# Attention inside a transformer block: the first 160 queries of a weighted sum moved ahead of the third score product, and the accumulator copied in pieces of 160 and 352

## The chip, the cores and the metric

The kernel runs on one core of one Trainium2 chip. The core has a matrix engine (TensorE, in the profile PE, with its weight loads as PEld), VectorE (DVE), ScalarE (ACT), GpSimd (POOL) and SyncE (SP), which issues transfers. Each works off its own list of instructions in order, and waits for the others through semaphores. The metric is the device time of one execution in microseconds. Lower is better.

## What is computed

```
def _A_ref(x, wqkv, wo):                 # B=1, S=2048, D=512
    H = 32; Dh = D // H                  # 32 heads of 16
    q, k, v = ...                        # (x @ wqkv), by heads
    scores = einsum("bhqd,bhkd->bhqk", q, k) * Dh ** -0.5
    p = softmax(scores, axis=-1)
    o = einsum("bhqk,bhkd->bhqd", p, v)
    return o.transpose(0, 2, 1, 3).reshape(B, S, D) @ wo

h  = x + _A_ref(_layernorm(x))
h2 = h + _B_ref(_layernorm(h))           # a gated MLP with a 2048x2048 mix of the rows
```

The change lies in the attention, between the projections and `@ wo`.

## The kernel before

The attention stage goes through *units*: one group of four heads (`hg`, 8 of them), one block of 512 queries (`qb`, 4) and one block of 128 keys (`kb`, 16). Two units make a *pair*, the body of the main loop (line 1044, `n` in steps of two), 256 pairs in all. The first 246 follow a fixed order, the list `PAIR` of line 40 (the last of them without the products M below); the others, at the end of the stage, take another branch.

A pair interleaves three streams on TensorE:

- **Score products s0 to s7** (line 804): transposed scores of one head, 128 keys by 512 queries, into one of three `s` buffers in PSUM (the matrix engine's accumulation memory). ScalarE takes the exponential of each into `pt` (line 813). With three buffers, a score product needs the exponential of the third one before it to have ended. s0 to s3 belong to the first unit, s4 to s7 to the second, each by two head pairs and two heads. They run in the order s0, s2, s1, s3, s5, s4, s6, s7.
- **Products for the row maxima M0 to M7** (line 223): the same scores the other way round, for a block of queries some eleven pairs ahead. Softmax needs each row's maximum before its exponentials. They run in the order M0, M4, M1, M2, M3, M5, M7, M6 and take four PSUM banks in turn, `m0` to `m3`, by `count[0] % 4`: M0 and M3 share the first, M4 and M5 the second, M1 and M7 the third, M2 and M6 the fourth. VectorE takes the maximum of each (line 228), but M3's absolute value is taken by ScalarE (line 233) and joined with M6's on VectorE (line 237, one instruction that adds and takes the maximum).
- **Weighed sums** (`weigh`, line 824): the exponentials times the values, into the accumulator `pv`, one PSUM bank of 128 rows and 512 queries, as four products side by side, one for each head, in 32 columns of the array each. The fp32 operands make each product two passes, so a group of four shows as eight instructions. `P` is the sum of the pair's first unit, all 512 queries, at the end of the pair. The sum of the second unit follows in the next pair in two halves of 256 queries, both called `H` in the list (H1 and H2 below); it reads the exponentials of s4 to s7 of the previous pair.

A *boundary pair* is the first of a block of queries (`kb == 0`). After its H2 the accumulator holds the finished block. At the token `out` the function `take` (line 836) copies it on VectorE to `og` in SBUF and sends it to memory in two transfers. P of the same pair begins the next block in the same bank. 30 boundary pairs run the list `PAIR`; the first pair of all has no block before it.

Three tokens do smaller things: `join` (the maxima of a finished block are put together, on VectorE and GpSimd), `turn` (they are transposed on VectorE and go through memory into the queries' tile, three transfers, line 255) and `invert` (the reciprocal of the sums of a block, line 772). Each comes once in eight pairs, none in a boundary pair.

TensorE, ScalarE, VectorE, GpSimd and SP keep the order in which the program names their instructions, so the list is the order of TensorE's queue. The framework places the waits.

Of the kernel before, what the change touches and what calls it, by code (L numbers as in the profile page):

```python
# [8 lines left out]
F32 = mybir.dt.float32  # L9
# [6 lines left out]
AX = mybir.AxisListType  # L16
# [3 lines left out]
P = 128  # L20
# [16 lines left out]
FIRST = 2  # L37
RG = 64
VW = DH + 1
PAIR = "s0 M0 join s2 M4 M1 s1 H s3 invert M2 s5 M3 H out M5 s4 M7 turn s6 s7 M6 P".split()  # L40
HF = 3 * P
FC = FH // 2
LOW = -3.0e38
# [16 lines left out]
def block_kernel(ctx: ExitStack, tc: tile.TileContext, x, wqkv, wo, w_in, w_sp4, b_sp, w_out, out):  # L60
# [134 lines left out]
                    qst[g][RG * t + j:RG * t + KS:3, :, :],  # L195
                    q_scr[(0, 1, 0)[j], h0:h0 + 2 * DH, c].rearrange("(p r) s -> r p s", r=DH))

    more = {}

    def bank(i):  # L200
        if i in more:
# [3 lines left out]
    def max_pair(m):  # L205

        g, i = divmod(m, 8)
        hg, qb = divmod(g, NQ)
        q, k, w = qst[g], kst[hg % 2], uvs[hg % 2]
        if i == 0:
            mx[g] = sm.tile([P, 16, 4], F32, name="mx")
            nc.gpsimd.memset(mx[g][:, :8, 3:], LOW)
        c, p = slice(i % 4 * P, i % 4 * P + P), i // 4
        at = lambda t, e: mx[g][:, t * 8 + i, e:e + 1]

        def scores(t, keys, b):  # L220
            r = slice(RG * t, RG * t + KS)
            acc = bank(b)
            nc.tensor.matmul(acc, q[r, p, c], keys[r, p], start=True, stop=True)  # L223
            return acc

        def one(t, e, b):
            acc = scores(t, k[:, :, 512 * e:512 * e + 512], b)
            nc.vector.reduce_max(at(t, e if t else e - 1), acc, axis=AX.X)  # L228

        def minus(b):  # L230
            acc = scores(0, w[:, :, 512:], b)
            ab[0] = sm.tile([P, 512], F32, name="ab")
            nc.scalar.activation(ab[0], acc, AF.Abs)  # L233

        def plus(b):
            acc = scores(0, w[:, :, :512], b)
            nc.vector.tensor_tensor_reduce(ab[0], acc, ab[0], 0.5, LOW, ALU.add, ALU.max, at(0, 0))  # L237

        def finish():
            if i == 7:  # L240
                nm = sm.tile([P, 2, 8], F32, name="nm")
                nc.vector.tensor_reduce(nm.rearrange("p t i -> p (t i)"), mx.pop(g), axis=AX.X,  # L242
                                        op=ALU.max, negate=True)
                parts = sm.tile([P, 2, 2, 8], F16, name="mparts")
                nc.gpsimd.tensor_scalar(nm, nm, 1.0 / ONE, 1.0, op0=ALU.mult, op1=ALU.mult)  # L245
                nc.gpsimd.tensor_copy(parts[:, :, 0], nm)
                nc.gpsimd.tensor_sub(parts[:, :, 1], nm, parts[:, :, 0])
                turned[0] = (g, parts)

        ab = {}  # L250
        four = [lambda b, e=e: one(1, e, b) for e in range(4)]
        two = [lambda b, e=e: one(0, e, b) for e in (2, 3)]
        return [four[0], two[0], two[1], minus, four[1], four[2], plus, four[3], finish]

# [532 lines left out]
    with ExitStack() as at:  # L787
# [36 lines left out]
        def weigh(hg, qb, kb, a=0, b=512):  # L824
            if kb == 0:
                pv[0] = ps_v.tile([P, 512], F32, name="pv")
            for j in range(4):
                c = (4 * kb + j) * VW
                nc.tensor.matmul(pv[0][32 * j:32 * j + 32, a:b], vst[hg % 2][:, c:c + 32],  # L829
                                 pts[j % 2, kb][:, j // 2, a:b], start=kb == 0, stop=kb == NB - 1,  # L830
                                 skip_group_check=True)
            if b == 512:
                for p in range(2):
                    del pts[p, kb]

        def take(hg, qb, pool=sm):

            o = pool.tile([P, 512], F32, name="og", bufs=2)
            nc.vector.tensor_copy(o, pv[0])  # L839
            for t in range(2):  # L840
                nc.sync.dma_start(four_heads(o_scr, hg)[t, :, :, qb * 512:qb * 512 + 512],
                                  o[64 * t:64 * t + 64])
# [201 lines left out]
        for n in range(0, len(units), 2):  # L1044
            (hg, qb, kb), (_, _, kb1) = units[n:n + 2]
            if m % 8 and n < 480:
                work(4.1 if m % 8 < 7 else 2.0)
            if n == 480:
                work(None)
            if hg + 1 < HG and n % 64 < 24 and n % 4 == 0:  # L1050
                load_k(hg + 1, [n % 64 // 4])
            if hg + 1 < HG and n % 64 < 12 and n % 4 == 2:
                load_uv(hg + 1, [n % 64 // 4])
            if hg + 1 < HG and n % 64 == 30:
                copy_v = load_v(hg + 1)
            if hg + 1 < HG and n % 64 == 36:
                copy_v()
            if kb == 2 and n // NB + 3 < HG * NQ:
                load_q(n // NB + 3)
            steps = max_pair(m) if m < 8 * HG * NQ else []  # L1060
            m += 1
            if not steps and not later:
                maxima.close()
                later.append(attn.enter_context(
                    tc.tile_pool(name="ps_l", bufs=1, space=PSUM, side="right")))
                steps_h.append(make_h(h_rows[0], later[0].tile([P, 512], F32, name="h")))
            elif not steps and len(later) == 1:
                inner.close()
                later.append(at.enter_context(tc.tile_pool(name="ps_t", bufs=2, space=PSUM)))
            ends = kb == 0 and n  # L1070

            def join():
                if joins:
                    joins.pop()()

            def some_h(k):
                for _ in range(k):
                    if steps_h and next(steps_h[0], True):
                        steps_h.pop()

            if kb == 2 and n > NB:
                gather_sums(*units[n - 3][:2])
            if len(later) == 2:
                if turned:
                    max_rows()
                more_h = n in (492, 494, 508, 510)
                scores2(hg, qb, kb, 0)
                scores2(hg, qb, kb, 1)
                some_h(1 + more_h)
                weigh(*prev)  # L1090
                if ends:
                    take(*prev[:2])
                scores2(hg, qb, kb1, 0)
                scores2(hg, qb, kb1, 1)
                some_h(1)
                weigh(hg, qb, kb)
            first = True
            for tok in PAIR if len(later) < 2 else ():
                i = int(tok[-1]) if tok[-1].isdigit() else 0
                if tok[0] == "s":  # L1100
                    score(hg, qb, (kb, kb1)[i // 4], i % 4 // 2, i % 2)
                elif tok[0] == "M" and steps:
                    steps[i](count[0] % 4)
                    count[0] += 1
                    if i == 6:
                        joins.append(steps[8])
                elif tok == "join":
                    join()
                elif tok == "H" and prev is None:
                    if first:  # L1110
                        pv[0] = ps_v.tile([P, 512], F32, name="pv")
                        for j in range(4):
                            nc.tensor.matmul(pv[0][32 * j:32 * j + 32, :], vst[0][:, :32],
                                             vst[0][:, :512], start=True, stop=True)
                    first = False
                elif tok == "H":
                    a = 0 if first else 256
                    weigh(*prev, a, a + 256)
                    first = False
                elif tok == "P":  # L1120
                    weigh(hg, qb, kb)
                elif tok == "out" and ends:
                    take(*prev[:2])
                elif tok == "invert" and kb == 6 and n > NB:
                    invert()
                elif tok == "turn" and turned:
                    max_rows()
            prev = (hg, qb, kb1)
            if len(later) == 2 and kb == 6:
                invert()  # L1130
            if n in (474, 484, 504, 508):
                asked.append(load_o(h_rows[{474: 0, 484: 1, 504: 2, 508: 3}[n]]))
            if n in (484, 492, 508):
                asked.pop(0)()
            if len(later) == 1 or n in (498, 510):
                split_o(h_rows[{498: 1, 510: 2}.get(n, 0)], False)
            if n == 500:
                steps_h.append(make_h(h_rows[1], later[0].tile([P, 512], F32, name="h")))
            if n == 502:
                new_hn(h_rows[0])  # L1140
# [458 lines left out]
```

## Time and profile before

| | us |
|---|---|
| three runs | 1713.01, 1713.76, 1713.85; median 1713.76 |
| the profiled execution | 1713.42 |
| its span, first to last instruction | 1711.6 |
| busy: PE, DVE, ACT, POOL | 1699.2, 1452.3, 1317.3, 811.9 |

The profiled execution has 1.8 us around its span. The granted clock of TensorE is full all along. The page divides the span into 40 slices of 42.8 us; these lines give the busy share of each in tenths, and the attention in the order of `PAIR` is the stretch from the fifth to the 29th:

```profile
DVE  7688999999999999999999999999936787543444
ACT  4334999999999999999999999999995545211111
PEclk9999999999999999999999999999999999999999
```

A row of a group names line, engine, operation, output and inputs and how often, then the busy time and the mean duration of one in ns, then the engine's idle time before them and what ended it. A row of a timeline gives the start in us from the span's beginning, the duration in us, engine, line and operation, and the count of those that follow one another. Durations on one engine overlap: the next instruction starts while the last is still finishing, so the step from start to start (or from end to end) is what one more instruction costs. The ends of matrix products are modelled.

### The profile page before, as it was taken

Reading aid. Unit: us, or ns where it says so; the run is one execution under the profiler, and the core shown is the slowest. Engines: PE = TensorE matmul, PEld = TensorE weight load, DVE = VectorE, ACT = ScalarE, POOL = GpSimd, SP = SyncE. Lnnn points to the kernel's source line nnn. Section 1 sums busy time; section 2 is a strip of 40 time slices with the busy share of each in tenths; the row PEclk is TensorE's granted clock in tenths of the full one; section 3 lists DMA queues with packets and bytes.
Section 4 is the critical chain, followed back from the end, with each engine's and each line's share of the span. In section 5 each row is a group of like instructions: output and inputs, shape, how many; then the busy total and the mean of one; then the engine's idle time right before and its main releaser. Section 6 shows DMA issues by size and latency. Waiting matters only on the chain.

```text
span 1711.6 us, 36671 instructions
## 1 busy us (share of the span) xinstructions
PE 1699.2 (99%) x13499; PEld 643.8 (38%) x13499; DVE 1452.3 (85%) x3051; ACT 1317.3 (77%) x2584; POOL 811.9 (47%) x1062
## 2 busy tenths in 40 slices
PE   9999999999999999999999999999999999999999
PEld 4533222222222222222222222222225666656665
DVE  7688999999999999999999999999936787543444
ACT  4334999999999999999999999999995545211111
POOL 1231867776673267687667776400002766300100
PEclk9999999999999999999999999999999999999999
DMA  5534332332221244344434444300114454664551
GB/s 185 163 98 142 105 89 67 102 94 81 82 66 24 57 118 117 98 150 126 130 113 123 132 140 130 80 13 19 37 39 124 139 174 139 235 234 156 199 216 44
DMA packets 189309, 196.03 MB, mean 115 GB/s; under 512 B 67496, under 2 KB 140008, under 8 KB 189128
## 3 DMA queue, kind: packets, MB, share of 16 engines
q1 hardware_dynamic: 186824, 188.04, 37.1%
q10 hardware_dynamic: 2304, 5.64, 0.8%
q8 instruction: 106, 1.74, 0.4%
q14 instruction: 75, 0.61, 0.1%
HBM read 122.10 MB, written 65.93 MB: 110 GB/s over the span
## 4 chain that ended last, share of the span: by engine, by line
PE 77%; DVE 13%; DMA 3%; POOL 3%; SPq 2%; ACT 1%; issue 1%; DVEq 0%; ACTq 0%; POOLq 0%
PE pv L829 26%; PE s L804 17%; PE m L223 9%; DVE mx L228 7%; PE g L108 4%; PE g L109 4%; PE g L107 4%; PE acc L107 4%; PE acc L109 3%; PE acc L108 3%; DMA rc<-r_scr 2%; DVE ab L237 1%; DVE og L839 1%; SPq L722 1%; DMA raw<-in_w_sp 1%
## 5 line engine op out<-in xcount | busy, mean ns | idle before, releaser
L813 ACT ACTIVATE pt<-s 128x512 f32<-128x512 f32 x1968 | 1007.1, 638 | 4.7 <-PE m L223 3.6
L228 DVE TENSOR_REDUCE mx<-m 128x1 f32<-128x512 f32 x1510 | 946.8, 681 | 11.8 <-PE m L223 2.9
L804 PE MATMUL s<-qst,kst 50*128 50x512 f16 x2048 | 604.2, 379 | 0.2
L829 PE MATMUL pv<-pt,vst 128*32 128x256 f32 (+1 forms) x6056 | 598.2, 466 | 4.0 <-DVE og L839 1.3
L223 PE MATMUL m<-kst,qst 48*128 48x512 f16 x1510 | 452.3, 381 | 0.0
L804 PEld LDWEIGHTS <-kst 50*128 50x128 f16 x2048 | 131.8, 94 | 352.0 <-issue 322.8
L829 PEld LDWEIGHTS pv<-pt,vst 128*32 128x32 f32 x6056 | 119.5, 108 | 289.4 <-issue 276.1
L223 PEld LDWEIGHTS <-qst 48*128 48x128 f16 x2048 | 159.3, 93 | 174.2 <-issue 124.6
L223 PE MATMUL m<-uvs,qst 48*128 48x512 f16 x504 | 190.7, 380 | 0.0
L245 POOL TENSOR_SCALAR nm<-nm 128x16 f32<-128x16 f32 x32 | 6.5, 203 | 358.3 <-DVE nm L242 358.3
L237 DVE CUSTOM_DVE_ANT_0 ab<-m,ab 128x512 f32<-128x512 f32 x252 | 170.2, 675 | 2.7 <-ACT ab L233 2.7
L233 ACT ACTIVATE ab<-m 128x512 f32<-128x512 f32 x252 | 157.8, 626 | 15.6 <-PE m L223 14.8
L1367 ACT ACTIVATE pr<-pr,up 128x304 f32<-128x304 f32 (+1 forms) x32 | 17.0, 574 | 108.5 <-DVE up L1321 108.5
L990 POOL TENSOR_TENSOR op<-raw,op 128x512 f16<-128x512 f32 x80 | 92.8, 1160 | 6.1
L913 POOL TENSOR_TENSOR raw<-raw 128x512 f32<-128x512 f32 (+1 forms) x84 | 83.1, 989 | 6.7
L918 POOL TENSOR_TENSOR acc_sp<-acc_sp,raw 128x512 f32<-128x512 f32 x63 | 80.3, 1275 | 4.5
L109 PE MATMUL acc<-wi,hT 128*128 128x344 f16 x256 | 79.1, 309 | 0.3 <-DVE hT L104 0.3
L107 PE MATMUL acc<-wi,hT 128*128 128x344 f16 x256 | 79.1, 309 | 0.0
L108 PE MATMUL acc<-wi,hT 128*128 128x344 f16 x256 | 79.1, 309 | 0.0
L1506 POOL TENSOR_TENSOR pr<-pr,z 128x344 f32<-128x344 f32 x8 | 7.3, 910 | 145.9 <-DMA whole<-squares 108.3
L910 POOL TENSOR_SCALAR raw<-raw 128x512 f32<-128x512 f32 (+1 forms) x88 | 52.1, 592 | 19.7 <-DMA raw<-in_wqkv 12.4
L1505 DVE TENSOR_TENSOR pr<-g,v 128x344 f32<-128x344 f32 x8 | 4.1, 516 | 66.6 <-PE g L109 63.5
(247 smaller groups left out, 2288.5 us busy)
## 6 DMA issues: line engine op xcount, KB each, us to landing
raw<-in_w_sp SPq DMA_DIRECT2D x128, 256.0 KB
s_scr<-op SPq DMA_DIRECT2D x64, 256.0 KB
op<-s_scr SPq DMA_DIRECT2D x32, 512.0 KB
a_scr<-op SPq DMA_DIRECT2D x48, 256.0 KB
op<-a_scr SPq DMA_DIRECT2D x24, 512.0 KB
o_scr<-og SPq DMA_DIRECT2D x64, 128.0 KB
qst<-q_scr SPq DMA_DIRECT2D x192, 32.0 KB
kst<-k_scr SPq DMA_DIRECT2D x48, 128.0 KB
```

Source lines behind the costliest of these rows:

```text
L107: nc.tensor.matmul(ps, lh, rh, start=first, stop=False, **kw)
L108: nc.tensor.matmul(ps, lh, rl, start=False, stop=False, **kw)
L109: nc.tensor.matmul(ps, ll, rh, start=False, stop=last, **kw)
L223: nc.tensor.matmul(acc, q[r, p, c], keys[r, p], start=True, stop=True)
L228: nc.vector.reduce_max(at(t, e if t else e - 1), acc, axis=AX.X)
L233: nc.scalar.activation(ab[0], acc, AF.Abs)
L237: nc.vector.tensor_tensor_reduce(ab[0], acc, ab[0], 0.5, LOW, ALU.add, ALU.max, at(0, 0))
L804: nc.tensor.matmul(s, kst[hg % 2][r, p, kb * P:(kb + 1) * P], qst[hg * NQ + qb][r, p, :], start=True, stop=True)
L813: nc.scalar.activation(pts[p, kb][:, t, :], s, AF.Exp, scale=scales_[hg // 2])
L829: nc.tensor.matmul(pv[0][32 * j:32 * j + 32, a:b], vst[hg % 2][:, c:c + 32], pts[j % 2, kb][:, j // 2, a:b], start=kb == 0, stop=kb == NB - 1,
L913: pool.tensor_mul(got[0] if n else acc, got[0], got[0])
L990: chores.append((lambda: pool.tensor_sub(t[0][:, 1], of(), t[0][:, 0]), TT))
```

## The change

Four edits.

- The list: the first part H1 goes from behind s1 to ahead of it, directly behind s2 and M4; M1 goes from ahead of s1 to behind it; `turn` goes from behind M7 to ahead of M5, and `invert` from behind s3 to behind `turn`.
- The two parts of the second unit's sum are 160 and 352 queries instead of 256 and 256, in every pair.
- In a boundary pair the accumulator is copied in two pieces: 160 queries directly behind H1, 352 at `out` behind H2. The transfers follow the second piece.
- In a boundary pair the maximum of M2 is held: it is not issued behind its product but behind the second piece, at `out`.

```
-PAIR = "s0 M0 join s2 M4 M1 s1 H s3 invert M2 s5 M3 H out M5 s4 M7 turn s6 s7 M6 P".split()
+PAIR = "s0 M0 join s2 M4 H s1 M1 s3 M2 s5 M3 H out turn invert M5 s4 M7 s6 s7 M6 P".split()
...
         def one(t, e, b):
             acc = scores(t, k[:, :, 512 * e:512 * e + 512], b)
-            nc.vector.reduce_max(at(t, e if t else e - 1), acc, axis=AX.X)
+            to = at(t, e if t else e - 1)
+            if hold:
+                held.append(lambda: nc.vector.reduce_max(to, acc, axis=AX.X))
+            else:
+                nc.vector.reduce_max(to, acc, axis=AX.X)
...
-        def take(hg, qb, pool=sm):
-
-            o = pool.tile([P, 512], F32, name="og", bufs=2)
-            nc.vector.tensor_copy(o, pv[0])
+        def take(hg, qb, pool=sm, a=0, b=512):
+
+            if not a:
+                pv[1] = pool.tile([P, 512], F32, name="og", bufs=2)
+            o = pv[1]
+            nc.vector.tensor_copy(o[:, a:b], pv[0][:, a:b])
+            if b < 512:
+                return
...
                 elif tok[0] == "M" and steps:
+                    if ends and i == 2:
+                        hold.append(1)
                     steps[i](count[0] % 4)
+                    hold.clear()
...
                 elif tok == "H":
-                    a = 0 if first else 256
-                    weigh(*prev, a, a + 256)
+                    weigh(*prev, *((0, 160) if first else (160, 512)))
+                    if ends and first:
+                        take(*prev[:2], a=0, b=160)
                     first = False
...
                 elif tok == "out" and ends:
-                    take(*prev[:2])
+                    take(*prev[:2], a=160)
+                    while held:
+                        held.pop(0)()
```

More of the change, by code (lines that the diff above doesn't have):

```diff
@@ L196, in load_q @@
                     q_scr[(0, 1, 0)[j], h0:h0 + 2 * DH, c].rearrange("(p r) s -> r p s", r=DH))
-    more = {}
+    more, hold, held = {}, [], []
     def bank(i):
```

## Prediction

> **What bounds the kernel now.** I read the page first (its groups), then the attention stage, pair by pair, in the timelines of ScalarE, TensorE and VectorE. In the groups, ScalarE's exponentials and VectorE's maxima are the two largest:
>
> ```profile
> L813 ACT ACTIVATE pt<-s 128x512 f32<-128x512 f32 x1968 | 1007.1, 638 | 4.7 <-PE m L223 3.6
> L228 DVE TENSOR_REDUCE mx<-m 128x1 f32<-128x512 f32 x1510 | 946.8, 681 | 11.8 <-PE m L223 2.9
> 197.47:1227.36 1029.89, 1025.96 (x9282) 291.50 (x9280) 1022.06 (x1984) 1028.59 (x2089) 613.10 (x809) 1.00 0.33 91
> ```
>
> The last row is a window that begins at one first exponential of a boundary pair and ends at another, 232 pairs later: 1029.89/232 = 4.439 us a pair. Its busy columns are TensorE, weight loads, VectorE, ScalarE, GpSimd; all three main engines look full, so the shares do not tell which one sets the pace. Single rows do. Durations overlap (an operation starts before the last has ended), so I compare ends. A regular pair, its first and its last exponential:
>
> ```profile
> 783.33 0.66 ACT L813 ACTIVATE pt<-s 128x512 f32<-128x512 f32 x1
> 783.82 0.66 ACT L813 ACTIVATE pt<-s 128x512 f32<-128x512 f32 x1
> 787.74 0.66 ACT L813 ACTIVATE pt<-s 128x512 f32<-128x512 f32 x1
> ```
>
> The first row is the last exponential (s7) of the pair before and ends at 783.99; s0 ends at 784.48, this pair's s7 at 788.40. Eight operations lie between the last two (seven exponentials and one absolute value), so (788.40 - 784.48)/8 = 0.49 us each, and the step 783.99 to 784.48 is 0.49 too. Nine times 0.49 is 4.41: in a regular pair ScalarE finishes one operation every 0.49 us without a hole. **ScalarE is the bound**, and no order of the others makes a regular pair shorter than 4.41. ScalarE loses time only around a boundary, where a new block of queries begins:
>
> ```profile
> 769.88 0.66 ACT L813 ACTIVATE pt<-s 128x512 f32<-128x512 f32 x1
> 770.56 0.60 ACT L813 ACTIVATE pt<-s 128x512 f32<-128x512 f32 x1
> 774.39 0.69 ACT L813 ACTIVATE pt<-s 128x512 f32<-128x512 f32 x1
> 775.06 0.60 ACT L813 ACTIVATE pt<-s 128x512 f32<-128x512 f32 x1
> ```
>
> These are s7 of the boundary pair, s0 of the next pair, that pair's s7, and the s0 after it. Ends 770.54 to 771.16 are 0.62 apart, 775.08 to 775.66 are 0.58: 0.13 and 0.09 more than 0.49. So a boundary costs 0.22 us, and the 30 boundaries that run this order cost 6.6 us. That is all that the reordered stage can give back. Why they cost it is seen on TensorE and VectorE:
>
> ```profile
> 765.55 0.39 PE L804 MATMUL s<-qst,kst 50*128 50x512 f16 x1
> 766.19 0.37 PE L804 MATMUL s<-qst,kst 50*128 50x512 f16 x1
> 767.06 0.39 PE L804 MATMUL s<-qst,kst 50*128 50x512 f16 x1
> 767.29 0.38 PE L804 MATMUL s<-qst,kst 50*128 50x512 f16 x1
> 767.60 0.64 PE L829 MATMUL pv<-pt,vst 128*32 128x256 f32 x8
> 768.64 0.39 PE L223 MATMUL m<-uvs,qst 48*128 48x512 f16 x1
> 769.14 1.07 PE L829 MATMUL pv<-pt,vst 128*32 128x512 f32 x8
> 770.14 0.39 PE L804 MATMUL s<-qst,kst 50*128 50x512 f16 x1
> 766.01 0.69 DVE L228 TENSOR_REDUCE mx<-m 128x1 f32<-128x512 f32 x1
> 766.61 0.68 DVE L228 TENSOR_REDUCE mx<-m 128x1 f32<-128x512 f32 x1
> 767.21 0.68 DVE L228 TENSOR_REDUCE mx<-m 128x1 f32<-128x512 f32 x1
> 767.81 0.68 DVE L228 TENSOR_REDUCE mx<-m 128x1 f32<-128x512 f32 x1
> 768.41 0.68 DVE L839 COPY og<-pv 128x512 f32<-128x512 f32 x1
>   DVE og L839: 10.9, 30
> ```
>
> On TensorE: s0, s1, s3, s5, the second half H2 of the weighed sum, M6, the whole product P, then s0 of the next pair. On VectorE: the maxima of M0, M4, M1, M2 and the copy of the accumulator. P overwrites the accumulator, so it waits for the copy: 768.41 + 0.68 = 769.09, P at 769.14. The last line is from the view of what waited for `pv`: 30 such waits, 10.9 us of idle time. In the second pair another wait decides:
>
> ```profile
> 772.61 0.68 DVE L228 TENSOR_REDUCE mx<-m 128x1 f32<-128x512 f32 x1
> 773.34 0.37 PE L223 MATMUL m<-uvs,qst 48*128 48x512 f16 x1
> 773.64 1.06 PE L829 MATMUL pv<-pt,vst 128*32 128x512 f32 x8
> 774.64 0.39 PE L804 MATMUL s<-qst,kst 50*128 50x512 f16 x1
> ```
>
> The maximum of M2, here late behind the copy, ends at 773.29, and M6 goes at 773.34, 0.05 later. By the code M2 and M6 use the same bank (the fourth and the eighth product of a pair, four banks). M6 late makes P late (0.30 behind it), s0 late (1.00 behind P) and s0's exponential late (774.64 to 775.06: 0.42). **This wait is the one to watch**: the change moves exactly M2's maximum.
>
> **The change part by part, in the times of that boundary pair.** *The first part of the sum, now ahead of s1.* It reads the exponential of the previous s7, which s1 waited for before (s7's buffer is the one s1 needs). So its last product goes at 766.19, where s1 went, and s1 comes behind it. Duration of the part: the rows
>
> ```profile
> 784.04 0.37 PE L804 MATMUL s<-qst,kst 50*128 50x512 f16 x1
> 784.34 0.64 PE L829 MATMUL pv<-pt,vst 128*32 128x256 f32 x8
> 784.91 0.39 PE L804 MATMUL s<-qst,kst 50*128 50x512 f16 x1
> ```
>
> give 0.57 from the start of 256 queries to the next score, and P gives 1.00 for 512 (773.64 to 774.64): 1.68 ns a query and 0.14 fixed. So 160 take 0.41 and 352 take 0.73, together the 1.14 of two halves: TensorE's work does not change. In every pair, s1 now comes 0.05 + 0.41 = 0.46 after the end of exponential s7 (784.04 against 783.99 is the 0.05), and its own exponential can end 0.42 + 0.60 later, at 1.48, where ScalarE would be ready to end it at 3 x 0.49 = 1.47. That is a stall of 0.01 in each of 215 regular pairs (245 less 30), 2.2 us. If only the last of the four column products waits and the three others have gone, some 0.02 are saved and the stall is nothing. I take the middle, 1.1 us. A gain is excluded by ScalarE's 0.49. From above: if 160 queries took as long as 256, 0.57, the stall would be 0.17 a pair, 37 us; I take the line through two rows since both have the same form. s3 now follows s1 at once instead of behind the half, which gives it room, and s0 of the next pair keeps its place, since the sum of the parts is the same.
>
> *The copy in two pieces.* A step on VectorE is 0.60 for 512 elements. The nearest small operation is in the trace with its successor:
>
> ```profile
> 611.17 0.21 DVE L242 TENSOR_REDUCE nm<-mx 128x16 f32<-128x64 f32 x1
> 611.29 0.68 DVE L228 TENSOR_REDUCE mx<-m 128x1 f32<-128x512 f32 x1
> ```
>
> 64 elements take a step of 0.12, so 0.48 for 448 more: 1.07 ns each and 0.05 fixed. A piece of 160 steps 0.22, one of 352 0.43; 0.65 instead of 0.60. Bounds: no fixed part (0.17 and 0.38), or 0.60 each.
>
> *Where the pieces stand.* VectorE: M0 766.01, M4 766.61, first piece 767.21, M1 767.43, free at 768.03. The first piece ends 0.08 behind its step (0.68 against 0.60), at 767.51. H2 writes other columns of the tile that this piece reads. Its own place: s5 could go at 766.19 + 0.41 + 2 x 0.23 = 767.06 (the 0.23 from 767.06 to 767.29), but its buffer is free only when exponential s2 has ended, two steps behind s7 (766.19 - 0.05 + 2 x 0.49 = 767.12), so 767.17; H2 0.31 later (767.29 to 767.60), 767.48. If it waits for the first piece, as P does for the whole copy, 767.57. The trace of before has no read between two writes of one accumulator, so both are bounds; I take the wait, the nearer to P's row.
>
> [...]
>
> *H2, the second piece and M2's maximum.* A group of 256 lasts 0.64 to its end, so 352 last 0.80: H2 ends at 768.37. The copy follows the last product by 0.06 where VectorE waits for it:
>
> ```profile
> 1292.00 1.38 PE L829 MATMUL pv<-pt,vst 128*32 128x512 f32 x7
> 1293.44 0.69 DVE L839 COPY og<-pv 128x512 f32<-128x512 f32 x1
> ```
>
> So the second piece starts at 768.43: VectorE, free at 768.03, stands idle for 0.40, because M2's maximum is held behind the piece. That maximum then starts at 768.86, ends at 769.54, and M6 goes at 769.59, where it went at 768.64. P follows at 769.89 (before 769.14), s0 at 770.89 (770.14), its exponential at 771.31 (770.56). **ScalarE loses 0.75 more** in each boundary. What P waited for is indeed gone (the second piece ends at 768.94), but M6, ahead of P, goes 0.95 later. Nothing hides it: behind M6 on TensorE are P and the next pair's s0 and s2, the only work that ScalarE could take, and s7, ahead of M6, is its last.
>
> In the next pair VectorE has caught up: M5, M7 and M6 run at 769.46, 770.06 and 770.66, free at 771.27, before the next M0 can be there (770.89 + 0.42 = 771.31). M2's maximum ends there at 771.31 + 3 x 0.60 + 0.68 = 773.79; M6's turn comes 3.09 behind s0 (765.55 to 768.64), at 773.98. So the second loss of 0.09 goes. Net 0.75 - 0.09 = 0.66 a boundary, 30 x 0.66 = 19.8 us.
>
> [...]
>
> *`turn` and `invert`.* Each once in eight pairs, in pairs that are no boundary. Turn's transpose steps ahead of M5's maximum and needs GpSimd's three small operations:
>
> ```profile
> 612.02 0.22 POOL L247 TENSOR_TENSOR mparts<-nm,mparts 128x16 f16<-128x16 f32 x1
> 614.35 0.20 DVE L259 STREAM_TRANSPOSE mturned<-mparts 128x32 f16<-128x32 f16 x1
> ```
>
> They end at 612.24; VectorE would come to the transpose after M2's maximum, about 613.1. So no wait; 0.9 is the cover. If that were gone, M5's, M7's and M6's maxima behind it would be late, for which no product of the same pair waits. Its three transfers are issued on SP in the same order, a microsecond earlier, behind the output's two. Invert moves 0.16 of VectorE from before M2's maximum to behind it, and its two transfers move some 2 us back on SP; its regular pair is 4.41 already. Both at nothing.
>
> **Sum.** The profiled execution took 1713.42 (span 1711.6 and 1.8 around it), 0.34 under the median 1713.76. 1713.42 + 19.8 + 1.1 = 1734.3, and as a median 1734.6.
>
> **The rivals.** *Faster: M6 is not late.* If M2's maximum did not hold M6 (another bank, or the held maximum ending by 768.59), P would go 0.30 after M6, at 768.94, or 0.05 after the second piece, 768.99, before the 769.14 of now. With all losses gone the time is 1713.4 - 6.6 = 1706.8. It decides where the maximum starts by 767.91; against it stands that H2 itself ends no earlier than 768.28. Chance 0.07. *About the same:* the held maximum costs only what the copy cost, 0.22; P might then go 0.09 later than now and M6 no later than 768.93, against 769.45 with every bound at its best. 1713.8, chance 0.05. *Every pair pays:* if the part ahead of s1 costs more than 0.41, each 0.01 is 2.2 us on top; at 0.49, midway to the bound, 1734.6 + 17 = 1752. For it: the margin is 0.01. Against: two rows of the same form give the line. Chance 0.08.
>
> **How the numbers follow.** The forecast has 0.80. Its low end has pieces without fixed part and H2 without a wait: H2 ends 768.28, the piece starts 768.34, the maximum 768.72, M6 769.45: 0.52 net, 15.6 us and no loss in regular pairs, 1729. Its high end has 0.60 a piece: first piece to 767.89, H2 767.94, second piece 768.80, maximum 769.40, M6 770.13: 1.20 net, 36 us, 1752. I cut that, since a piece costs less than the whole, and reach below 1729 for boundaries that hide a part: 1720 to 1748 holds most of the forecast and part of the pairs' case. This kernel's measurement tells 0.2% (3.4 us) from no change: faster 0.07, same 0.05, slower 0.88.
>
> **What would show it.** In the changed profile: M6 of a boundary pair waiting for a maximum (line 228's successor) and no longer P for `og`; ScalarE's gap between s7's and s0's ends near 1.37 instead of 0.62, and 0.49 in the pair after; VectorE idle about 0.4 before the second piece; eight pairs taking 8 x 4.439 + 0.66 = 36.17; regular pairs at 4.41 to 4.42. I am wrong if M6 goes by 768.6 in such a pair, if regular pairs leave 4.41 by more than 0.02, or if H2's column count costs other than 1.68 ns.

## The result, and the profile after

| | us |
|---|---|
| before, beside the changed kernel | 1713.8 (1713.01 to 1714.18, 4 runs) |
| changed | 1734.16 (1733.43 to 1734.47, 4 runs) |
| ratio | 1.012, 95% interval 1.0107 to 1.0132 |
| the profiled execution's span | 1711.6 before, 1732.5 changed |

The change made the kernel slower by 20.4 us; 1734.6 was predicted. Lines have moved in the changed kernel: the maxima are line 232, the held one line 230, the copies line 845, scores 808, sums 833, exponentials 817.

The page and a view of one window of the changed kernel show the size of it. The window runs, as the one of before, from the first exponential of a boundary pair to another 232 pairs and 29 boundaries later (columns after the length: busy time of TensorE, weight loads, VectorE, ScalarE and GpSimd, then the granted clock, the DMA's busy share and GB/s):

```profile
L817 ACT ACTIVATE pt<-s 128x512 f32<-128x512 f32 x1968 | 1005.2, 630 | 29.1 <-PE m L223 29.0
L223 PE MATMUL m<-uvs,qst 48*128 48x512 f16 x504 | 191.4, 381 | 14.7 <-DVE mx L230 14.7
197.85:1248.78 1050.93, 1034.75 (x9282) 324.27 (x9280) 1025.31 (x2013) 1026.52 (x2090) 612.99 (x809) 1.00 0.32 90
```

The window is 1050.93 - 1029.89 = 21.04 us longer, 0.73 a boundary. The first two lines already name cause and effect: the products from `uvs` (M3 and M6) now have 14.7 us of idle TensorE ahead of them, all of it ended by line 230, and ScalarE is idle 29.1 us ahead of exponentials, where it was 4.7. (The page puts ScalarE's waits down to line 223, because in the trace scores (line 808) and maxima products (line 223) count up the same semaphore, number 102, and the exponential waits for that one; what it reads, by the code, is the score issued beside that product.)

The boundary pair in the timeline of TensorE, from s0 to the next pair's s0:

```profile
777.47 0.39 PE L808 MATMUL s<-qst,kst 50*128 50x512 f16 x1
778.49 0.39 PE L808 MATMUL s<-qst,kst 50*128 50x512 f16 x1
779.52 0.80 PE L833 MATMUL pv<-pt,vst 128*32 128x352 f32 x8
781.57 0.37 PE L223 MATMUL m<-uvs,qst 48*128 48x512 f16 x1 [0.49 <-DVE mx L230]
781.87 1.06 PE L833 MATMUL pv<-pt,vst 128*32 128x512 f32 x8
782.87 0.39 PE L808 MATMUL s<-qst,kst 50*128 50x512 f16 x1
```

and of VectorE, with the first maxima, the two pieces and the held maximum:

```profile
777.96 1.28 DVE L232 TENSOR_REDUCE mx<-m 128x1 f32<-128x512 f32 x2
779.16 0.32 DVE L845 COPY og<-pv 128x160 f32<-128x160 f32 x1
779.39 0.68 DVE L232 TENSOR_REDUCE mx<-m 128x1 f32<-128x512 f32 x1
780.39 0.52 DVE L845 COPY og<-pv 128x352 f32<-128x352 f32 x1 [0.32 <-PE pv L833]
780.83 0.68 DVE L230 TENSOR_REDUCE mx<-m 128x1 f32<-128x512 f32 x1
```

The rows of TensorE are s0, s1, H2, M6, P and the next pair's s0. Read upward from M6: it goes at 781.57, 0.05 after the held maximum ended (780.83 + 0.68 = 781.51, the rest is rounding). That maximum stands behind the second piece, which waited for H2; and H2 went at 779.52, 0.04 to 0.05 after the first piece ended (779.48). Behind M6 come P (+0.30) and the next s0 (+1.00). ScalarE, around it:

```profile
777.38 0.67 ACT L817 ACTIVATE pt<-s 128x512 f32<-128x512 f32 x1
781.79 0.67 ACT L817 ACTIVATE pt<-s 128x512 f32<-128x512 f32 x1
783.29 0.60 ACT L817 ACTIVATE pt<-s 128x512 f32<-128x512 f32 x1 [0.83 <-PE m L223]
787.12 0.69 ACT L817 ACTIVATE pt<-s 128x512 f32<-128x512 f32 x1
787.65 0.64 ACT L817 ACTIVATE pt<-s 128x512 f32<-128x512 f32 x1
```

The s7 of the pair before ends at 778.05 and the boundary pair's s7 at 782.46, 4.41 later: inside the boundary pair nothing is lost. The next s0 ends at 783.89, 1.43 after that, 0.94 more than a step of 0.49. The next pair's s7 and the s0 behind it (787.81 and 788.29) are 0.48 apart, the ordinary step to the rounding: the second loss of before is gone. Regular pairs did not move: two first exponentials, one pair apart,

```profile
796.48 0.64 ACT L817 ACTIVATE pt<-s 128x512 f32<-128x512 f32 x1
800.89 0.64 ACT L817 ACTIVATE pt<-s 128x512 f32<-128x512 f32 x1
```

are 4.41 apart. In the 29 blocks of the window, measured from the end of one first exponential to the next one's, a boundary pair takes 5.36 on average (4.56 before), the pair behind it 4.41 (4.48 before), and each of the six others 4.41 to 4.43 in both.

### The profile page after: what moved, and what is told of

It reads as the page before. It is cut to its first block, busy times and chain, and to the rows that moved or that the text cites. A ratio compares the mean times of both kernels' runs of the same rounds, so it can differ in the third digit from the quotient of the medians.

```text
span 1732.5 us, 36701 instructions
## 1 busy us (share of the span) xinstructions
PE 1708.6 (99%) x13499; PEld 679.5 (39%) x13499; DVE 1455.0 (84%) x3081; ACT 1315.4 (76%) x2584; POOL 811.4 (47%) x1062
## 4 chain that ended last, share of the span: by engine, by line
PE 83%; DVE 10%; ACT 2%; DMA 2%; issue 1%; SPq 1%; POOL 0%; ACTq 0%; DVEq 0%; POOLq 0%
PE pv L833 31%; PE s L808 21%; PE m L223 8%; PE g L108 4%; PE g L109 4%; PE g L107 4%; PE acc L107 3%; DVE mx L232 3%; PE acc L109 3%; PE acc L108 3%; DVE og L845 1%; DMA rc<-r_scr 1%; DVE mx L230 1%; DVE rs_t L124 1%; DVE rs_u L126 1%
## 5 line engine op out<-in xcount | busy, mean ns | idle before, releaser
L817 ACT ACTIVATE pt<-s 128x512 f32<-128x512 f32 x1968 | 1005.2, 630 | 29.1 <-PE m L223 29.0
L232 DVE TENSOR_REDUCE mx<-m 128x1 f32<-128x512 f32 x1480 | 934.3, 682 | 21.2 <-PE m L223 3.3
L833 PE MATMUL pv<-pt,vst 128*32 128x352 f32 (+2 forms) x6056 | 612.1, 466 | 1.8
L808 PE MATMUL s<-qst,kst 50*128 50x512 f16 x2048 | 597.7, 380 | 0.4
L223 PEld LDWEIGHTS <-qst 48*128 48x128 f16 x2048 | 163.3, 93 | 242.5 <-issue 215.2
L833 PEld LDWEIGHTS pv<-pt,vst 128*32 128x32 f32 x6056 | 133.3, 108 | 237.0 <-issue 189.2
L223 PE MATMUL m<-uvs,qst 48*128 48x512 f16 x504 | 191.4, 381 | 14.7 <-DVE mx L230 14.7
```

The costliest lines, as they stand in the source:

```text
L232: nc.vector.reduce_max(to, acc, axis=AX.X)
L808: nc.tensor.matmul(s, kst[hg % 2][r, p, kb * P:(kb + 1) * P], qst[hg * NQ + qb][r, p, :], start=True, stop=True)
L817: nc.scalar.activation(pts[p, kb][:, t, :], s, AF.Exp, scale=scales_[hg // 2])
```

## The experiments

Three questions: is it the hold, and not the pieces or the order; is it the bank; and how near to a loss are the regular pairs. Net losses a boundary below come from the same window, 232 pairs and 29 boundaries, against the 1029.89 us of before. The kernel before ran beside the first four at 1713.56 us and beside the last two at 1713.52 us.

**The hold alone.** The kernel before, with the held maximum as the only edit.

```
+                    if ends and i == 2:
+                        hold.append(1)
                     steps[i](count[0] % 4)
+                    hold.clear()
...
                 elif tok == "out" and ends:
                     take(*prev[:2])
+                    while held:
+                        held.pop(0)()
```

> The kernel before with one edit of the change alone: in a boundary pair M2's maximum is issued behind the (whole) copy. Theory (M6 waits for the held maximum, its bank is M2's): H2 ends at 768.24 in the times of before, the copy starts at 768.30 and the maximum at 768.90, M6 goes at 769.63 instead of 768.64; s0's exponential 0.80 later, the loss of 0.09 in the next pair gone: 0.70 a boundary, 21 us, 1734.8 us. Rival (the cost is in the split of the copy and in H2 waiting for the first piece): neither is here, 1713.8 us. Rival (every pair pays for the new order and the parts of 160 and 352): neither is here, 1713.8 us.

Measured: 1734.28 us (ratio 1.0122, interval 1.0105 to 1.0139). The window:

```profile
196.99:1247.37 1050.38, 1031.95 (x9282) 290.74 (x9280) 1027.86 (x1984) 1026.44 (x2090) 612.98 (x809) 1.00 0.33 90
```

The timeline of TensorE and VectorE in a boundary pair (the copy is line 843 here):

```profile
778.29 0.64 PE L833 MATMUL pv<-pt,vst 128*32 128x256 f32 x8
778.99 0.69 DVE L843 COPY og<-pv 128x512 f32<-128x512 f32 x1 [0.41 <-PE pv L833]
779.60 0.68 DVE L230 TENSOR_REDUCE mx<-m 128x1 f32<-128x512 f32 x1
780.33 0.37 PE L223 MATMUL m<-uvs,qst 48*128 48x512 f16 x1 [0.64 <-DVE mx L230]
```

20.49/29 = 0.71 a boundary, where 0.70 was expected, and the same picture: VectorE idle until H2 has ended, then the copy, then the maximum, then M6. One edit of the four, without the new order and without pieces, gives the whole loss.

**The change without the hold.**

```
                 elif tok[0] == "M" and steps:
-                    if ends and i == 2:
-                        hold.append(1)
                     steps[i](count[0] % 4)
```

> The changed kernel without the hold: M2's maximum runs behind its product, between the maximum of M1 and the second piece; list, parts and pieces as changed. Theory: M6 is on time, P waits for the second piece as it waited for the copy, which now ends a little later (0.24 lost in the boundary pair, 0.09 in the next): 0.33 a boundary instead of 0.22, 1717 us. Rival (pieces and H2's wait): most of the 20 us stay, about 1732 us. Rival (every pair pays): 1734 us.

Measured: 1715.36 us (ratio 1.0011, interval 1.0001 to 1.002). The window:

```profile
197.98:1230.60 1032.62, 1028.17 (x9282) 320.54 (x9280) 1020.01 (x2013) 1028.44 (x2089) 612.96 (x809) 1.00 0.34 91
```

The timeline of VectorE and TensorE in a boundary pair:

```profile
769.39 1.28 DVE L232 TENSOR_REDUCE mx<-m 128x1 f32<-128x512 f32 x2
770.59 0.51 DVE L845 COPY og<-pv 128x352 f32<-128x352 f32 x1
770.72 0.37 PE L223 MATMUL m<-uvs,qst 48*128 48x512 f16 x1
771.16 1.06 PE L833 MATMUL pv<-pt,vst 128*32 128x512 f32 x8
```

M2's maximum (the second of the two at 769.39) fills the time in which VectorE stood idle; M6 does not wait, and P waits for the second piece (it ends at 770.59 + 0.51 = 771.10, P goes at 771.16), as it waited for the copy before. 2.73/29 = 0.09 a boundary net, 0.11 expected. The two-piece copy with H2's wait costs little, and the rival that puts the 20 us there falls.

**Order and parts alone.** The run above, with the copy whole and at its old place.

```
-                    if ends and first:
-                        take(*prev[:2], a=0, b=160)
...
-                    take(*prev[:2], a=160)
+                    take(*prev[:2])
```

> The changed kernel with list and parts of 160 and 352 as changed, but the copy whole at its old place and no hold. Theory: regular pairs at 4.41 still, 0.25 a boundary, 1714.5 us. Rival (every pair pays for the order and the parts): 1734 us. Rival (pieces): 1713.8 us, the same here as the theory.

Measured: 1714.44 us (ratio 1.0006, interval 0.9996 to 1.0015), not to be told from before. Its window is

```profile
197.71:1228.47 1030.76, 1025.79 (x9282) 322.07 (x9280) 1018.14 (x1984) 1028.45 (x2089) 613.12 (x809) 1.00 0.33 91
```

0.87 us longer than before's, 0.03 a boundary. So the 245 pairs pay nothing for the part ahead of s1, and none of these edits gives back the losses of before either.

**Another bank for M6.** The changed kernel with M3 and M2 exchanged in the list; the bank follows the place.

```
-PAIR = "s0 M0 join s2 M4 H s1 M1 s3 M2 s5 M3 H out turn invert M5 s4 M7 s6 s7 M6 P".split()
+PAIR = "s0 M0 join s2 M4 H s1 M1 s3 M3 s5 M2 H out turn invert M5 s4 M7 s6 s7 M6 P".split()
```

> The changed kernel, hold and pieces kept, with M3 and M2 changing places in the list: M3 beside s3, M2 beside s5. The banks go by turns, so M6 now follows M3 (freed by ScalarE) and M2 shares its bank with M0. Theory: M6 no longer waits for the held maximum and P goes about when the second piece has ended, ScalarE loses 0.04 there; but VectorE is behind by some 0.8, M0's maximum makes the next pair's M2 late and 0.41 is lost in that pair: 0.45 a boundary, 1720.6 us; in the boundary pair M6 directly behind s7. Rival (the hold costs by VectorE's order alone, whatever the bank): 1734 us.

Measured: 1811.11 us (ratio 1.0571). The total is 90 us off. What the run was made for did come: in a boundary pair

```profile
862.32 0.90 PE L808 MATMUL s<-qst,kst 50*128 50x512 f16 x2
862.67 0.68 DVE L230 TENSOR_REDUCE mx<-m 128x1 f32<-128x512 f32 x1
862.85 0.39 PE L223 MATMUL m<-uvs,qst 48*128 48x512 f16 x1
863.17 1.06 PE L833 MATMUL pv<-pt,vst 128*32 128x512 f32 x8
```

M6 goes at 862.85, beside s7 (the second of the two scores, which end at 863.22), while the held maximum still runs until 863.35, 0.50 later. It does not wait for it any more, with the hold in place: the wait hangs on the bank. But every pair now takes 4.84 (1122.88/232, the window below). I had moved the absolute value, which goes with M3, ahead of exponential s5 on ScalarE, and s7 needs the buffer that s5's exponential frees. The window, and behind it the timeline of a regular pair:

```profile
201.51:1324.39 1122.88, 1055.38 (x9282) 297.87 (x9280) 1037.60 (x2012) 1047.42 (x2088) 611.67 (x807) 1.00 0.31 84
```

```profile
866.52 0.63 ACT L237 ACTIVATE ab<-m 128x512 f32<-128x512 f32 x1
867.00 0.64 ACT L817 ACTIVATE pt<-s 128x512 f32<-128x512 f32 x1
867.69 0.37 PE L808 MATMUL s<-qst,kst 50*128 50x512 f16 x1 [0.24 <-ACT pt L817]
868.01 1.06 PE L833 MATMUL pv<-pt,vst 128*32 128x512 f32 x8
```

s5's exponential ends at 867.64, s7 goes 0.05 later, and M6, P and the next s0 stand behind it: s7 holds the same queue that M6 held. Boundary pairs take 4.84 too, so in so long a pair the boundary costs nothing on top, and the expected 0.45 a boundary was not tried by this run.

**A larger part ahead of s1.** Order of the change, whole copy, no hold, parts of 224 and 288.

```
-                    weigh(*prev, *((0, 160) if first else (160, 512)))
+                    weigh(*prev, *((0, 224) if first else (224, 512)))
```

> The run with the whole copy and no hold (order of the change), with parts of 224 and 288 queries instead of 160 and 352. The work is the same; only s1 comes later behind the end of exponential s7. Theory (from the line of 1.68 ns a query): the part takes 0.52 instead of 0.41, s1 is due 0.05 + 0.52 - 0.02 = 0.55 after that end, where 0.45 is the latest that ScalarE allows: 0.10 a regular pair, regular pairs at 4.51, 215 pairs, 21 us on top of 1714.4: 1735.5 us. Rival (ScalarE has more room than worked out, the place and size of the part do not matter): 1714.4 us and regular pairs at 4.41.

Measured: 1731.36 us (ratio 1.0104, interval 1.0087 to 1.0121). The timeline of ScalarE, s2 and s1 in a regular pair, and the window:

```profile
794.61 0.65 ACT L817 ACTIVATE pt<-s 128x512 f32<-128x512 f32 x1
795.26 0.60 ACT L817 ACTIVATE pt<-s 128x512 f32<-128x512 f32 x1
```

```profile
198.44:1245.38 1046.94, 1042.67 (x9282) 311.95 (x9280) 1030.45 (x1983) 1046.87 (x2089) 612.75 (x808) 1.00 0.33 90
```

The ends are 0.60 apart, 0.11 over the step where 0.10 was expected. The window is 16.18 us longer than with 160, though 203 regular pairs at 0.10 would make 20. The expectation left out the pairs around a boundary: in this trace the regular pairs of a block take 4.50 to 4.51, 0.09 to 0.10 more than with 160, but the pair behind a boundary pair takes 4.49 (4.48 with 160) and the boundary pair itself 4.56 (4.60 with 160), so there the stall falls into time that ScalarE loses anyway. So 160 has a real edge beside it: 64 queries more cost 17 us.

**M6 behind P in the boundary pairs.** The changed kernel, hold and pieces kept.

```
-            for tok in PAIR if len(later) < 2 else ():
+            last_m6 = PAIR[:-2] + ["P", "M6"]
+            for tok in (last_m6 if ends and steps else PAIR) if len(later) < 2 else ():
```

> The changed kernel, hold and pieces kept, with M6 behind P instead of ahead of it, in the boundary pairs alone. Theory: P then waits for the second piece only and goes 0.6 earlier, but s0 stands behind M6, which no longer shares its time with a score, and VectorE is still behind by its idle time before the second piece: in the boundary pair 0.30 is lost instead of 0.94, in the next pair M0's maximum is late by some 0.8, M6 there waits for M2's maximum again and 0.43 is lost: 0.73 a boundary, 1734 us, the same time with the loss in two places. Rival (M6 ahead of P in the queue is the whole cost, and moving it aside is enough): 0.3 a boundary at most, 1716.5 us.

Measured: 1727.45 us (ratio 1.0082, interval 1.0065 to 1.0099). The timeline of ScalarE, s7 of the boundary pair and the next s0, then the same one pair later, and the window:

```profile
778.37 0.67 ACT L817 ACTIVATE pt<-s 128x512 f32<-128x512 f32 x1
779.23 0.60 ACT L817 ACTIVATE pt<-s 128x512 f32<-128x512 f32 x1 [0.19 <-PE m L223]
783.06 0.69 ACT L817 ACTIVATE pt<-s 128x512 f32<-128x512 f32 x1
784.08 0.60 ACT L817 ACTIVATE pt<-s 128x512 f32<-128x512 f32 x1 [0.33 <-PE m L223]
```

```profile
197.90:1242.61 1044.71, 1042.47 (x9282) 321.46 (x9280) 1022.53 (x2013) 1029.54 (x2090) 612.99 (x809) 1.00 0.33 90
```

Ends 779.04 to 779.83, 0.30 over the step; 783.75 to 784.68, 0.44 over it. Both losses are the expected ones (0.30 and 0.43), in the expected places. The total was not: I had set their sum, 0.73, beside the changed kernel's net 0.73, though it is a gross figure; less the 0.22 that before loses it is 0.51, and the window says 14.82/29 = 0.51. In the second pair the wait is again that for M2's maximum (the timeline of VectorE and TensorE):

```profile
781.62 0.68 DVE L232 TENSOR_REDUCE mx<-m 128x1 f32<-128x512 f32 x1
782.35 0.37 PE L223 MATMUL m<-uvs,qst 48*128 48x512 f16 x1
```

So with M6 out of P's way 0.51 of the 0.73, some 70% of the loss, remains. By the code VectorE still has the two copies and the held maximum behind the second piece in the boundary pair (0.32 idle ahead of that piece in the changed kernel), and in the pair behind it M2's maximum ends at 782.30 and M6 goes at 782.35: the loss comes back at the next bank.

## Why the prediction was right

**The bound.** ScalarE's 0.49 an operation held: the regular pairs of the changed kernel take 4.41, as before, and no version's median was below the kernel before. That ScalarE sets the 4.41 rests on its ends without a hole; no run took work off it.

**The wait.** As forecast, M6 waits for the held maximum, P and s0 stand behind it, and the second pair's loss goes. Shown three ways: alone it gives the whole loss, taken out nothing of it is left but 0.09 a boundary, and with another bank M6 goes while the maximum runs.

**H2 behind the first piece.** Taken as likely, not certain; H2 went 0.05 after the piece in all 30 boundaries of the changed kernel's trace; in the trace of before the sum behind a copy goes 0.05 after it 24 times of 31, and 0.15 after it the other seven. It is no wait by address: the piece reads columns 0 to 159, H2 writes 160 to 511. In the trace the first weight load of H2 (779.52) waits for the semaphore that VectorE's instructions count up, number 100, after 0.35 us of idle weight loads that the first piece ends; so it is one of the waits that the framework placed. No run tried H2 without it. In the changed kernel's view of the accumulator, first what its instructions waited for, then who did the waiting, and in the view of all waits (total, times, longest), stand

```profile
  DVE og L845: 10.9, 31
  PEld pv L833: 10.9, 31
```

```profile
DVE og L845 <- PE pv L833: 19.9, 31, 10.2
```

The first two are idle time of the weight loads ahead of a sum until a copy ended, 0.35 us each; ahead of H2's products TensorE itself stands still for only 0.06 us, since M3 ends at 779.47. The total is that of before, which the prediction put down to P as a whole (there 9.6 of the 10.9 us are of weight loads). In a boundary pair these are now waits of H2, and P, 0.30 behind M6, has none of its own. The third is VectorE waiting for H2 ahead of the second piece: less the one long wait, (19.9 - 10.2)/30 = 0.32 a boundary from the end of M1's maximum, and 0.40 from the step after its start (779.39 + 0.60 = 779.99 to 780.39), the 0.40 of the forecast.

**The prices.** The pieces step 0.23 (779.16 to 779.39) and 0.44 (780.39 to 780.83), forecast 0.22 and 0.43. From the first piece's start to the second's is 1.23 (forecast 1.22), from there to M6 1.18 (forecast 1.16).

**The sizes that were off,** both small. A boundary costs 0.73 net instead of 0.66: ScalarE's gap is 1.43, not 1.37, and eight pairs take 1050.93/29 = 36.24, not 36.17. VectorE comes to the first piece 0.67 after s1 (778.49 to 779.16) instead of 0.61; s1 is 0.02 earlier, and VectorE itself some 0.04 later, which the walk from the pair of before did not have. And the stall of 1.1 us in regular pairs does not exist: s1 comes 0.44 after s7's exponential has ended (778.05 to 778.49), under the 0.45 that ScalarE allows (an estimate from the prediction's rows, 3 x 0.49 - 0.42 - 0.60), the lower of the two bounds. The first is 30 x 0.07 = 2 us too little, the second 1.1 us too much; they cancel in part. With both put right the span would have grown by 30 x 0.73 = 21.9 us; it grew by 1732.5 - 1711.6 = 20.9, just the 19.8 + 1.1 of the forecast. The 1 us between lies outside the window: the rest of the program is some 0.1 us shorter than before (20.9 against 21.04), although the 30th boundary is in it, and no run shows why. So the mechanism and, to 0.07 us, the loss of a boundary were foreseen; that the total came within 0.4 us is in part luck.

**The rivals.** "Every pair pays" was near: at 160 the price is nothing, at 224 it is 0.10 a pair. "M6 is not late": in the run without the hold M6 is on time, but M2's maximum then stands ahead of the second piece, P waits on the copy again, and the run lies 1.8 us above before, not below it. The rival as it was put, M6 on time with the maximum behind the piece, stood only in the run with M3 first, whose long pairs hide what it is worth. No version tried gave back the 6.6 us of before.

## What to carry to other kernels

Before an instruction is put off, look at what its buffer is needed for next, and what stands in that queue behind the one that needs it; here one maximum, 0.68 us long, moved behind a copy, held a product that had a whole sum and the bound engine's next two inputs behind it. When several engines look full in every view, compare the ends of their operations: here they showed which engine has no hole in a regular pair (ScalarE, one end every 0.49 us), and that all a new order could give back were its holes at the boundaries, 0.22 us each. A stall moved out of the way (M6 behind P, 0.30 us lost instead of 0.94) came back at the next buffer (0.44 us in the next pair), where VectorE was still behind.

## What the runs showed of the hardware that was not expected

ScalarE's starts and ends run at two rates. In the changed kernel's pair after a boundary, the first exponential behind the hole (783.29, 0.60 long) and the eighth operation behind it (787.12, 0.69 long) start (787.12 - 783.29)/8 = 0.48 apart and end (787.81 - 783.89)/8 = 0.49 apart; the durations grow by the difference, from 0.60 to 0.69, though all are of the same size (128x512). No run shows why. The rows do show that 0.60 is one operation behind a hole, 0.49 the price of one more, and 0.69 is neither.

And s1 came 0.44 after the end of the last exponential that the part ahead of it reads, where 0.46 was worked out for a group that waits as a whole. The group does not. The timeline of TensorE, cut off at 778.09 and at 778.10, counts

```profile
778.01 0.34 PE L833 MATMUL pv<-pt,vst 128*32 128x160 f32 x3
778.01 0.41 PE L833 MATMUL pv<-pt,vst 128*32 128x160 f32 x4
```

Three of the four column products go before s7's exponential ends at 778.05, and the fourth, the one that reads it, 0.05 after that end. So it is the prediction's other case, in which only the last product waits.
